# Matmuls that nobody reads, beside the first batch of an attention and feed-forward kernel

## The chip, the cores and the metric

The kernel runs on one core of one Trainium2 chip. The metric is the device time of one execution in microseconds (us); the median over runs counts. Engines are called TensorE (PE in the profile, PEld for its weight loads), VectorE (DVE), ScalarE (ACT), GpSimd (POOL) and SyncE (SP, whose queue issues nearly all DMAs here).

## The reference: what is computed

Attention on 8 batches of 8 heads, 576 tokens and 64 dimensions, as the sum of a coarse part (mean over 4 tokens, full softmax over 144 positions) and a local part (a window of 3 tokens to each side), followed by a feed-forward network with a leaky activation on 4608 rows:

```python
q_d = q.reshape(B, H, Sd, 4, D).mean(axis=3)      # k_d, v_d alike; Sd = 144
out_up = np.repeat(sm_attn(q_d, k_d, v_d), 4, axis=2)
mask = np.abs(pos[:, None] - pos[None, :]) < 4
out_local = softmax(where(mask, scale * q @ k.T, -1e9)) @ v
x = (out_up + out_local).transpose(0, 2, 1, 3).reshape(B * S, H * D)   # 4608 x 512
h = x @ w_in                                      # 512 x 2048
out = (maximum(h, 0) + alpha * minimum(h, 0)) @ w_out                  # 2048 x 512
```

w_in, w_out and alpha arrive as float64 and are decoded on the chip.

## The kernel before

**Feed-forward network.** The rows are cut into 18 chunks of 256 and the 2048 hidden columns into 8 pairs of 128, which makes 144 steps. A step `s` has these parts: `hidden` (24 matmuls of 128x256 into the tile `h`, line 784, from high and low parts `xh`, `xl` of x and `wih`, `wil` of w_in), `slopes` on ScalarE (tiles `t`, `sh`, lines 799 and 801), `larger` (line 811 on VectorE, or the helper `add` of line 76 on GpSimd for the steps in `EARLY`), `split` into `gh` (ScalarE, line 816) and `gl` (GpSimd, helper `sub`, line 73), and `product` (12 matmuls of 128x512 into `o`, line 845). In steps 0 to 21 GpSimd does both `larger` and `gl`.

**Weights.** Blocks `fp` of w_in and w_out are loaded (`load_raw`, lines 159 and 163, tile `raw`) into three slots in turn and decoded in `make`: ScalarE `Abs` (line 197, tile `temp`), four VectorE operations (201, 202, 206, 207), a ScalarE copy to `wih`/`woh` (212, 216) and a VectorE difference `wil`/`wol` (220, 224).

**First batch** (`first_batch`). Four pairs of heads. Per pair: TensorE transposes q and k (line 447, tiles `f0T`, `f1T`), ScalarE copies them to `qb`, `kT`; TensorE computes nine windows of scores (lines 463 and 467, tile `fs`); VectorE does the softmax (503 to 510, tile `fp`); TensorE transposes it (515, `fpt`), ScalarE copies (`fpT`), TensorE multiplies with v (531, `fpv`), and VectorE adds the coarse part (534, `fxs`) and splits x (540, 541, `xh`, `xl`). The coarse part runs beside it (`fsum`, `fsd`, `down_probs` with tile `pT`, `fdv`).

**Later batches.** `down(b, hp)` is the coarse part of one head pair of batch b: six loads (`ld`, line 247), folds on GpSimd (line 76, tiles `ld`, `s2q`, `s2k`, `s2v`), then `flip` (265, `qkT`), `scores` (278, `s`), the softmax (`dnb`, `dp`, `drs`), `turn` (302, `pT`) and `weigh` (312, `pv`). `local(u, ...)` is the local part of a third of a batch, unit u from 3 on; it runs on VectorE (lines 614 to 676) with a share on GpSimd (650, tile `pv`) and an exponential on ScalarE (634, tile `lex`).

**What sets the order.** Everything before event time 14 (`LISTED`) is put in order by a scheduler that has its own cost model of all engines; the rest stands in the order of a list of event times. Each engine works through its queue in order. So a change of TensorE's work in the first part can move instructions on every engine there.

In PSUM there are two banks `po` (`ps_o`), two `ph` (`ps_h`), two `d`, one `q` and one `l`.

Of the kernel before, what the change touches and what calls it, by code (L numbers as in the profile page):

```python
# [49 lines left out]
LISTED = 14  # L50
JOINS = (0.04, 0.06)


@with_exitstack
def tile_attention_moe(ctx: ExitStack, tc: tile.TileContext, q, k, v, w_in, w_out, alpha, out):
# [40 lines left out]
    for tag in ("spare6", "spare7", "spare2", "spare3", "slot2", "slot3"):  # L96
        one.tile([128, 2048], F32, tag=tag, name=f"{tag}_place")
    make_identity(nc, ident)

    masks = {}  # L100
# [136 lines left out]
    def down(b, hp, t0, gap, early=False):  # L237
# [21 lines left out]
        def flip():  # L259
            if hp == 0:  # L260
                new_od(b)
            pt = st["pt"] = bank("d", f"qkT{nm}")
            for i, x in enumerate("qk"):
                for g in range(2):
                    nc.tensor.transpose(pt[:, (2 * i + g) * 72:(2 * i + g) * 72 + 72], sums[x][:, g], ident[:72, :72])

        def operands():
# [7 lines left out]
        def scores():  # L275
            sv = st["sv"] = bank("d", f"s{nm}")[:96, 0:432].rearrange("p (b c) -> p b c", b=3)
            for bl in range(3):
                nc.tensor.matmul(sv[:, bl, :], qd32[:, bl, :], st["kd"], start=True, stop=True)  # L278

        def peak():  # L280
# [18 lines left out]
        def turn(g):  # L299
            tp = st["tp", g] = bank("d", f"pT{nm}_{g}")  # L300
            for bl in range(3):
                nc.tensor.transpose(tp[:72, 96 * bl:96 * bl + 96], st["p"][:, bl, 72 * g:72 * g + 72], ident[:96, :96])  # L302
# [36 lines left out]
    def down_probs(b, hp, sv):  # L339
# [16 lines left out]
        for g in range(2):  # L356
            tp = bank("d", f"pT{nm}_{g}")
            for bl in range(3):
                nc.tensor.transpose(tp[:72, 96 * bl:96 * bl + 96], p[:, bl, 72 * g:72 * g + 72],
                                    ident[:96, :96])  # L360
            th = one.tile([72, 288], F32, tag=f"th{g}", name=f"th{nm}_{g}")
            nc.scalar.copy(th, tp[:72, 0:288])
            parts.append(th)
            yield
# [20 lines left out]
    def first_batch(st):  # L385
# [13 lines left out]
        unit = st.tile([128, 128], F32R, name="unit")  # L399
        nc.scalar.copy(unit, ident)  # L400
        qb = st.tile([128, NWIN, 2, WIN], F32, name="qb")
        nc.vector.memset(qb[0:64, :, 1, :], 0.0)
# [38 lines left out]
        def pair(hp):  # L441
            halves = [slice(64 * e, 64 * e + 64) for e in range(2)]
            for x in range(2):
                for t0, nt in ((0, 4), (4, 4)):
                    ps = ps_h.tile([128, 512], F32, tag="ph", name=f"f{x}T{hp}{t0}")[:, 0:72 * nt]
                    for i in range(nt):
                        nc.tensor.transpose(ps[:, 72 * i:72 * i + 72],
                                            qk[hp][:, x, t0 + i].rearrange("p h d -> p (h d)"), ident[:72, :72])
                    if x == 0:
                        for e, r in enumerate(halves):  # L450
# [7 lines left out]
            for part in ("sd", "ds")[EM[hp] == "b"]:  # L458
                if part == "s":
                    banks = []  # L460
                    for w0, nw in ((0, 7), (7, 2)):
# [3 lines left out]
                        for i in range(nw):  # L465
                            w = w0 + i
                            nc.tensor.matmul(ps[:, KEYS * i:KEYS * i + KEYS], qb[:, w].rearrange("p e i -> p (e i)"),
                                             kT[:, WIN * w:WIN * w + KEYS], start=False, stop=(i == nw - 1))
                        banks.append((w0, w0 + nw, ps[:, 0:KEYS * nw].rearrange("p (w j) -> p w j", j=KEYS)))
                else:  # L470
# [9 lines left out]
                    for x in range(2):  # L480
                        for g in range(2):
                            nc.tensor.transpose(ps[:, (2 * x + g) * 72:(2 * x + g) * 72 + 72], sums[x][:, g],
                                                ident[:72, :72])
                    for e, r in enumerate(halves):
                        nc.scalar.mul(qd[r, :, 48 * e:48 * e + 48].rearrange("p b (i g) -> p b i g", g=2),
                                      ps[r, 0:144].rearrange("p (g b i) -> p b i g", g=2, b=3), DSCALE)
# [25 lines left out]
            for w0, nw in ((0, 4), (4, 4), (8, 1)):  # L512
                ps = pair_bank(FPT[hp][w0 // 4], f"fpt{hp}{w0}")
                for i in range(nw):
                    nc.tensor.transpose(ps[:KEYS, 128 * i:128 * i + 128], p[:, w0 + i], ident)
                nc.scalar.copy(pT[:, w0:w0 + nw].rearrange("p w i -> p (w i)"), ps[:KEYS, 0:128 * nw])
            if EM[hp] == "a":
                th = yield from down_probs(0, hp, sd)
            po = bank("d", f"fdv{hp}")
            for g in range(2):  # L520
                for e, r in enumerate(halves):
                    pr = th[g].rearrange("p (b e a) -> p b e a", b=3, e=2)[:, :, e]
                    nc.tensor.matmul(po[r, 0:144].rearrange("p (b a) -> p b a", b=3), vd[:, e, g], pr,
                                     start=(g == 0), stop=(g == 1))
            odf = st.tile([128, SD], F32, tag="odf", name=f"fod{hp}")
            nc.scalar.copy(odf, po[:, 0:144])
            for w0, nw in ((0, 4), (4, 4), (8, 1)):
                ps = pair_bank(FPV[hp][w0 // 4], f"fpv{hp}{w0}")
                for i in range(nw):
                    for e, r in enumerate(halves):  # L530
                        nc.tensor.matmul(ps[r, WIN * i:WIN * i + WIN], vw[hp][:, w0 + i, e, :],
                                         pT[:, w0 + i, 64 * e:64 * e + 64], start=True, stop=True)
                xs = rest[:, hp, :] if w0 == 8 else st.tile([128, 256], F32, tag="xs", name=f"fxs{hp}{w0}")
                nc.vector.tensor_tensor(
# [502 lines left out]
```

## Time and profile before

| | |
|---|---|
| median of 3 runs | 983.98 us (982.16 to 987.89) |
| the profiled execution: device time | 982.8 us |
| its span, first to last instruction | 981.0 us |
| TensorE busy (942.9 us of the span) | 96% |
| VectorE busy (819.5 us) | 84% |
| ScalarE busy (555.3 us) | 57% |
| GpSimd busy (527.6 us) | 54% |
| mean granted TensorE clock | 0.976 |

"Span" is taken from the first to the last instruction; the device time is 1.8 us longer. Shares are means over the whole span; the first 100 us, to which most of the change belongs, look different from the rest, so they are read in windows of their own. In a window table each engine has its busy time and its number of instructions, then come the granted TensorE clock (1.00 is full), the DMA share and the rate.

### The profile page before, as it was taken

The numbers are of one execution on the slowest core, as the hardware profiler recorded it, in microseconds if no ns is written. First come the engines' busy times: TensorE is split into PE (matmuls) and PEld (weight loads), VectorE is DVE, ScalarE is ACT, GpSimd is POOL, SyncE is SP. The second block draws the span as 40 slices with busy tenths as digits, with TensorE's granted clock in tenths as the row PEclk, the third lists the DMA queues.
The fourth block names the chain that finished last, engine by engine and source line by source line (L and its number), as shares of the span: only waits on it lengthen the run. The fifth ranks groups of instructions, "written<-read, shape, count | busy, mean of one in ns | idle before, by whom it ended". The sixth has DMA issues, their size and how long they took to land.

```text
span 981.0 us, 17943 instructions
## 1 busy us (share of the span) xinstructions
PE 942.9 (96%) x6402; PEld 842.0 (86%) x6402; DVE 819.5 (84%) x1318; ACT 555.3 (57%) x1483; POOL 527.6 (54%) x642
## 2 busy tenths in 40 slices
PE   5878999999999999999999999999999999999998
PEld 4757887987888888989988899898899989999997
DVE  7999978888879999998889899899898889997111
ACT  4767776544645655556554655565556664544442
POOL 2055877787887546555537365555466633323221
PEclk9956999999999999999999999999999999999999
DMA  8946723132333322422322423332333321310000
GB/s 200 232 146 208 254 90 107 61 114 85 111 101 116 114 76 88 139 80 83 119 78 86 127 86 93 108 98 68 105 112 103 110 63 46 97 34 22 1 22 22
DMA packets 63197, 98.28 MB, mean 100 GB/s; under 512 B 23556, under 2 KB 28932, under 8 KB 63108
## 3 DMA queue, kind: packets, MB, share of 16 engines
q1 hardware_dynamic: 62916, 96.88, 32.8%
q8 instruction: 50, 0.82, 0.3%
q10 hardware_dynamic: 192, 0.26, 0.1%
q14 instruction: 39, 0.32, 0.1%
HBM read 87.67 MB, written 9.44 MB: 99 GB/s over the span
## 4 chain that ended last, share of the span: by engine, by line
PE 59%; DVE 11%; POOL 4%; ACT 3%; issue 2%; DMA 1%; SPq 0%; DVEq 0%; POOLq 0%
PE o L845 28%; PE h L784 27%; DVE lb L673 3%; DVE pv L670 2%; DVE qk L614 1%; PE s L278 1%; PE pv L312 1%; DVE t L811 1%; DVE ls L618 1%; PE xp L682 1%; POOL t L76 1%; PE pT L302 1%; DVE xf L698 1%; ACT t L799 1%; POOL gl L73 1%
## 5 line engine op out<-in xcount | busy, mean ns | idle before, releaser
L73 POOL TENSOR_TENSOR gl<-t,gh 128x512 fp32r<-128x512 f32 x144 | 186.3, 1294 | 323.4 <-ACT gh L816 303.3
L799 ACT ACTIVATE t<-h,slope 128x256 f32<-128x256 f32 x288 | 136.3, 473 | 128.8 <-PE h L784 105.7
L845 PE MATMUL o<-woh,gh 128*128 128x512 f32 x576 | 192.8, 405 | 2.5 <-ACT gh L816 1.1
L784 PE MATMUL h<-xh,wih 128*128 128x256 f32 x1152 | 188.0, 285 | 2.6 <-ACT sh L801 1.9
L845 PE MATMUL o<-wol,gh 128*128 128x512 f32 x576 | 185.7, 393 | 0.0
L845 PE MATMUL o<-woh,gl 128*128 128x512 f32 x576 | 185.4, 393 | 0.0
L784 PE MATMUL h<-xh,wil 128*128 128x256 f32 x1152 | 180.7, 279 | 0.0
L784 PE MATMUL h<-xl,wih 128*128 128x256 f32 x1152 | 180.5, 279 | 0.0
L784 PEld LDWEIGHTS h<-xh,wih 128*128 128x128 f32 x1152 | 162.8, 190 | 13.0 <-ACT sh L801 2.6
L816 ACT CAST gh<-t 128x512 fp32r<-128x512 f32 x144 | 89.5, 622 | 140.3 <-DVE t L811 81.6
L76 POOL TENSOR_TENSOR ld<-ld 72x256 f32<-72x256 f32 x168 | 131.9, 787 | 67.4 <-DMA ld<-in_q 64.8
L784 PEld LDWEIGHTS h<-xh,wil 128*128 128x128 f32 x1152 | 155.3, 190 | 0.3
L784 PEld LDWEIGHTS h<-xl,wih 128*128 128x128 f32 x1152 | 154.6, 190 | 0.1
L811 DVE TENSOR_TENSOR t<-h,t 128x512 f32<-128x512 f32 x114 | 78.3, 687 | 88.2 <-ACT h L803 87.8
L618 DVE TENSOR_REDUCE ls<-qk 128x12 f32<-128x768 f32 (+1 forms) x126 | 136.2, 1083 | 3.1
L845 PEld LDWEIGHTS o<-woh,gl 128*128 128x128 f32 x576 | 108.0, 188 | 24.0
L845 PEld LDWEIGHTS o<-wol,gh 128*128 128x128 f32 x576 | 108.0, 188 | 23.1 <-DVE temp L207 0.2
L673 DVE TENSOR_TENSOR lb<-lb,pv 128x384 f32<-128x384 f32 x202 | 114.0, 564 | 5.9
L845 PEld LDWEIGHTS o<-woh,gh 128*128 128x128 f32 x576 | 99.1, 188 | 18.9 <-issue 2.6
L803 ACT ACTIVATE h<-h,sign 128x256 f32<-128x256 f32 x228 | 100.2, 439 | 0.0
L670 DVE TENSOR_TENSOR pv<-v,lb 128x1152 f32<-128x1152 f32 x84 | 93.6, 1115 | 2.7
L614 DVE TENSOR_TENSOR qk<-k,qp 128x768 f32<-128x768 f32 (+1 forms) x78 | 84.0, 1078 | 4.6 <-ACT qp L607 4.6
(151 smaller groups left out, 1185.7 us busy)
## 6 DMA issues: line engine op xcount, KB each, us to landing
k<-in_k SPq DMA_DIRECT2D x41, 384.0 KB
v<-in_v SPq DMA_DIRECT2D x41, 384.0 KB
out<-sg SPq DMA_DIRECT2D x140, 64.0 KB
raw<-in_moe_w_in SPq DMA_DIRECT2D x16, 512.0 KB
raw<-in_moe_w_out SPq DMA_DIRECT2D x16, 512.0 KB
ld<-in_q SPq DMA_DIRECT2D x56, 144.0 KB
ld<-in_k SPq DMA_DIRECT2D x56, 144.0 KB
ld<-in_v SPq DMA_DIRECT2D x56, 144.0 KB
```

The lines of the kernel that those rows point to most:

```text
L73: nc.gpsimd.tensor_tensor(o, a, b, op=ALU.subtract)
L76: nc.gpsimd.tensor_tensor(o, a, b, op=ALU.add)
L614: nc.vector.tensor_tensor(st["pr"][:, :nd], window(tiles[u, "k"], half, d0, nd), st["qp", half].unsqueeze(1).to_broadcast([128, nd, 2, 192 ...
L618: nc.vector.tensor_reduce(out=st["s"][:, half, d0:d0 + nd, :].rearrange("p a b -> p (a b)"), in_=st["pr"][:, :nd].rearrange("p a h (t d) - ...
L670: nc.vector.tensor_tensor(st["pr"][:, :nd], window4(tiles[u, "v"], half, d0, nd), prob(half, d0, nd), op=ALU.mult)
L673: nc.vector.tensor_tensor(st["acc"], st["acc"], st["pr"][:, i], op=ALU.add)
L784: nc.tensor.matmul(ph[:, j], w[:, m, 128 * o:128 * o + 128], x[:, m, :], start=(i == 0), stop=(i == 11))
L799: nc.scalar.activation(t[:, j], hs[st][:, j], AF.Copy, scale=slope[:, f:f + 1])
L803: nc.scalar.activation(other[:, j], hs[st][:, j], AF.Copy, scale=sign[:, f:f + 1])
L811: nc.vector.tensor_tensor(gs[st], hs.pop(st), gs[st], op=ALU.max)
L816: nc.scalar.copy(gh, t)
L845: nc.tensor.matmul(outs[c][m], g[:, j, 128 * m:128 * m + 128], wo[w][n][:, o, :], start=(f == 0 and i == 0), stop=(f == NF - 1 and i == 2))
```

## The change

Matmuls are added whose results nobody reads. A helper writes them to the columns of a PSUM tile that the kernel doesn't use, with operands that lie there anyway. They are put behind (in `turn`: ahead of) the matmuls of the stages of the first batch and of `down(1, 0)`, and 16 longer ones stand ahead of the first transposes.

```diff
+FILL = 3
+    def turn_over(ps, used, times):
+        w, x = turner["now"]
+        n = min(512 - used, x.shape[-1])
+        for _ in range(times):
+            nc.tensor.matmul(ps[:, used:used + n], w, x[:, 0:n], start=True, stop=True)
 # down(), only for the second batch's first pair (early)
 def flip():        +    turner["now"] = wi[0][0][:, 0, 0:128], wi[0][0][:, 0, 0:256]
                    +    turn_over(pt, 288, FILL)            # after the transposes
 def scores():      +    turn_over(full, 432, 2 * FILL)      # after the matmuls
 def turn(g):       +    turn_over(tp, 288, FILL)            # before the transposes
 # first batch
 down_probs:        +    turn_over(tp, 288, FILL)            # twice a pair
 first_batch:       +    turner["now"] = unit, wmask.rearrange("p w j -> p (w j)")
 pair(hp):
+                    if (hp, x, t0) == (0, 0, 0):
+                        for _ in range(16):
+                            nc.tensor.matmul(full.rearrange("p (a n) -> p a n", a=4), unit,
+                                             unit.unsqueeze(1).to_broadcast([128, 4, 128]), start=True, stop=True)
                     # f0T, f1T: four times a pair
+                    turn_over(full, 288, FILL)
 fs, w0 == 7:       +    turn_over(ps, 256, FILL)
 fsum:              +    turn_over(ps, 288, FILL)
 fpt, w0 == 8:      +    turn_over(ps, 256, FILL)
 fdv:               +    turn_over(po, 256, FILL)
 fpv: three times   +    turn_over(ps, 256, FILL)
```

Built, this gives TensorE 187 matmuls more: 16 of 128x512, 72 of 128x256 and 84 of 128x224 in the first batch, and 9 of 128x224 and 6 of 128x80 in `down(1, 0)`. Nothing is taken out. The other engines have the same instructions as before, in another order. The rows below are the program's own order, in which lines of the changed kernel are higher by 1 to 32 than those of the profile before (L107 is `turn_over`, L877 the old 845, L816 the old 784, L291, L319 the old 278, 302); a number at the end of a tile's name is that tile's own.

TensorE's first rows, before and after:

```order
L447 MATMUL f0T00_209<-ident_75,fqk0_154 128x72 x4
L447 MATMUL f0T04_216<-ident_75,fqk0_154 128x72 x4
L463 MATMUL fs00_254<-wmask_139,unit_141 128x490
L463 MATMUL fs07_263<-wmask_139,unit_141 128x140
L447 MATMUL f1T00_223<-ident_75,fqk0_154 128x72 x4
L447 MATMUL f1T04_229<-ident_75,fqk0_154 128x72 x4
```

```order
L468 MATMUL f0T00_209<-unit_141 128x512 x16
L471 MATMUL f0T00_209<-ident_75,fqk0_154 128x72 x4
L471 MATMUL f0T04_235<-ident_75,fqk0_154 128x72 x4
L107 MATMUL f0T00_209<-wmask_139,unit_141 128x224 x3
L107 MATMUL f0T04_235<-wmask_139,unit_141 128x224 x3
L488 MATMUL fs00_285<-wmask_139,unit_141 128x490
L488 MATMUL fs07_294<-wmask_139,unit_141 128x140
L471 MATMUL f1T00_245<-ident_75,fqk0_154 128x72 x4
L107 MATMUL f1T00_245<-wmask_139,unit_141 128x224 x3
L471 MATMUL f1T04_254<-ident_75,fqk0_154 128x72 x4
L107 MATMUL f1T04_254<-wmask_139,unit_141 128x224 x3
```

The sixteen long matmuls stand first, and each group of transposes has three short ones behind it.

GpSimd's queue where step 0 begins, before and after (`t0` is the sum for step 0; `ld1_1`, `s2k1_1`, `s2v1_1` are folds of the second batch's second pair):

```order
L76 TENSOR_TENSOR s2k1_1_1194<-ld1_1_3_1125 72x2x64
L76 TENSOR_TENSOR ld1_1_5_1201<-ld1_1_5_1201 72x2x128
L76 TENSOR_TENSOR t0_1019<-sh0_1020,t0_1019 128x512
L76 TENSOR_TENSOR s2v1_1_1248<-ld1_1_4_1157 72x2x64
L76 TENSOR_TENSOR s2v1_1_1248<-ld1_1_5_1201 72x2x64
L73 TENSOR_TENSOR gl0_1033<-t0_1019,gh0_1032 128x512
```

```order
L77 TENSOR_TENSOR s2k1_1_1375<-ld1_1_3_1306 72x2x64
L77 TENSOR_TENSOR ld1_1_5_1385<-ld1_1_5_1385 72x2x128
L77 TENSOR_TENSOR s2v1_1_1435<-ld1_1_4_1338 72x2x64
L77 TENSOR_TENSOR s2v1_1_1435<-ld1_1_5_1385 72x2x64
L77 TENSOR_TENSOR t0_1191<-sh0_1192,t0_1191 128x512
L74 TENSOR_TENSOR gl0_1208<-t0_1191,gh0_1207 128x512
```

`t0` now stands behind both folds `s2v1_1`.

TensorE around step 2 and the first product, before and after (`pT1_0`, `pv1_0` belong to the second batch's first pair, `qkT1_1` to its second):

```order
L302 MATMUL pT1_0_0_1197<-ident_75,dp1_0_1090 72x96
L302 MATMUL pT1_0_1_1203<-ident_75,dp1_0_1090 72x96
L784 MATMUL h2_1095<-xh0_107,wih1_854 128x256 x4
L784 MATMUL h2_1095<-xh0_107,wil1_855 128x256 x4
L784 MATMUL h2_1095<-xl0_108,wih1_854 128x256 x4
L784 MATMUL h2_1095<-xh0_107,wih1_854 128x256 x4
L784 MATMUL h2_1095<-xh0_107,wil1_855 128x256 x4
L784 MATMUL h2_1095<-xl0_108,wih1_854 128x256 x4
L312 MATMUL pv1_0_1243<-th1_0_0_1210,s2v1_0_940 64x144 x2
L312 MATMUL pv1_0_1243<-th1_0_1_1212,s2v1_0_940 64x144 x2
L265 MATMUL qkT1_1_1332<-ident_75,s2q1_1_1120 128x72 x2
L265 MATMUL qkT1_1_1332<-ident_75,s2k1_1_1194 128x72 x2
```

```order
L291 MATMUL s1_0_1242<-kd1_0_1238,qd32_100 96x144
L107 MATMUL s1_0_1242<-wih0_73 128x80 x6
L107 MATMUL pT1_0_0_1378<-wih0_73 128x224 x3
L816 MATMUL h2_1276<-xh0_107,wih1_1026 128x256 x4
L816 MATMUL h2_1276<-xh0_107,wil1_1027 128x256 x4
L816 MATMUL h2_1276<-xl0_108,wih1_1026 128x256 x4
L816 MATMUL h2_1276<-xh0_107,wih1_1026 128x256 x4
L816 MATMUL h2_1276<-xh0_107,wil1_1027 128x256 x4
L816 MATMUL h2_1276<-xl0_108,wih1_1026 128x256 x4
L877 MATMUL o0_0_1320<-woh0_79,gh0_1207 128x512
L877 MATMUL o0_0_1320<-wol0_80,gh0_1207 128x512
```

`pT1_0`, `pv1_0` and `qkT1_1` have left the place ahead of the first product `o0`; they now stand among the product matmuls of steps 1 and 2, behind the first product.

More of the change, by code (lines that the diff above doesn't have):

```diff
@@ L98, in tile_attention_moe @@
     make_identity(nc, ident)
+    turner = {}
+    def turn_over(ps, used, times):
[3 more added lines that the diff above has]
+            nc.tensor.matmul(ps[:, used:used + n], w, x[:, 0:n], start=True, stop=True)
     masks = {}
@@ L265, in flip @@
                     nc.tensor.transpose(pt[:, (2 * i + g) * 72:(2 * i + g) * 72 + 72], sums[x][:, g], ident[:72, :72])
+            if early:
+                turner["now"] = wi[0][0][:, 0, 0:128], wi[0][0][:, 0, 0:256]
+                turn_over(pt, 288, FILL)
         def operands():
@@ L275, in scores @@
         def scores():
-            sv = st["sv"] = bank("d", f"s{nm}")[:96, 0:432].rearrange("p (b c) -> p b c", b=3)
+            full = bank("d", f"s{nm}")
+            sv = st["sv"] = full[:96, 0:432].rearrange("p (b c) -> p b c", b=3)
             for bl in range(3):
                 nc.tensor.matmul(sv[:, bl, :], qd32[:, bl, :], st["kd"], start=True, stop=True)
+            if early:
+                turn_over(full, 432, 2 * FILL)
         def peak():
@@ L300, in turn @@
             tp = st["tp", g] = bank("d", f"pT{nm}_{g}")
+            if early:
+                turn_over(tp, 288, FILL)
             for bl in range(3):
@@ L360, in down_probs @@
                                     ident[:96, :96])
+            turn_over(tp, 288, FILL)
             th = one.tile([72, 288], F32, tag=f"th{g}", name=f"th{nm}_{g}")
@@ L400, in first_batch @@
         nc.scalar.copy(unit, ident)
+        turner["now"] = unit, wmask.rearrange("p w j -> p (w j)")
         qb = st.tile([128, NWIN, 2, WIN], F32, name="qb")
@@ L444, in pair @@
                 for t0, nt in ((0, 4), (4, 4)):
-                    ps = ps_h.tile([128, 512], F32, tag="ph", name=f"f{x}T{hp}{t0}")[:, 0:72 * nt]
+                    full = ps_h.tile([128, 512], F32, tag="ph", name=f"f{x}T{hp}{t0}")
+                    ps = full[:, 0:72 * nt]
+                    if (hp, x, t0) == (0, 0, 0):
+                        for _ in range(16):
+                            nc.tensor.matmul(full.rearrange("p (a n) -> p a n", a=4), unit,
+                                             unit.unsqueeze(1).to_broadcast([128, 4, 128]), start=True, stop=True)
                     for i in range(nt):
@@ L468, in pair @@
                                              kT[:, WIN * w:WIN * w + KEYS], start=False, stop=(i == nw - 1))
+                        if w0:
+                            turn_over(ps, 256, FILL)
                         banks.append((w0, w0 + nw, ps[:, 0:KEYS * nw].rearrange("p (w j) -> p w j", j=KEYS)))
@@ L483, in pair @@
                                                 ident[:72, :72])
+                    turn_over(ps, 288, FILL)
                     for e, r in enumerate(halves):
@@ L515, in pair @@
                     nc.tensor.transpose(ps[:KEYS, 128 * i:128 * i + 128], p[:, w0 + i], ident)
+                if w0 == 8:
+                    turn_over(ps, 256, FILL)
                 nc.scalar.copy(pT[:, w0:w0 + nw].rearrange("p w i -> p (w i)"), ps[:KEYS, 0:128 * nw])
@@ L524, in pair @@
                                      start=(g == 0), stop=(g == 1))
+            turn_over(po, 256, FILL)
             odf = st.tile([128, SD], F32, tag="odf", name=f"fod{hp}")
@@ L532, in pair @@
                                          pT[:, w0 + i, 64 * e:64 * e + 64], start=True, stop=True)
+                turn_over(ps, 256, FILL)
                 xs = rest[:, hp, :] if w0 == 8 else st.tile([128, 256], F32, tag="xs", name=f"fxs{hp}{w0}")
```

## The prediction

> **What bounds the kernel now.** I began with the slices of the page, TensorE, VectorE and the granted clock (each digit is a fortieth of the span, 24.5 us):
>
> ```profile
> PE   5878999999999999999999999999999999999998
> DVE  7999978888879999998889899899898889997111
> PEclk9956999999999999999999999999999999999999
> ```
>
> From the fifth slice on TensorE is full; in the first four, where the change lies, VectorE is fuller than TensorE. Then I cut the span where the granted clock changes (busy us and number of instructions for each engine, then clock, DMA share, GB/s):
>
> ```profile
> 0.00:32.76 32.76, 20.41 (x105) 18.49 (x106) 25.27 (x51) 17.33 (x41) 5.59 (x26) 1.00 0.91 195
> 32.76:46.41 13.65, 12.18 (x149) 9.86 (x149) 11.96 (x27) 11.83 (x35) 0.00 (x0) 1.00 1.07 287
> 46.41:87.37 40.96, 32.62 (x210) 25.57 (x207) 40.60 (x67) 28.74 (x71) 16.07 (x14) 0.50 0.48 158
> 94.20:97.61 3.41, 3.41 (x21) 3.18 (x20) 3.41 (x6) 1.46 (x3) 3.41 (x4) 0.50 0.91 282
> 97.61:230.70 133.09, 127.97 (x860) 112.98 (x856) 114.11 (x172) 84.41 (x230) 106.81 (x122) 1.00 0.38 125
> 230.70:250.00 19.30, 18.97 (x124) 17.31 (x125) 16.43 (x30) 8.05 (x26) 14.24 (x19) 0.91 0.22 67
> ```
>
> The clock is at half for 40.96 us of the first batch and for 3.41 us more. The 1.00 of the first row isn't believed, since the same score matmuls (first row below, 18 in 4.11 us) take 1.33 us for 10 once the clock is granted:
>
> ```profile
> 12.98 4.11 PE L467 MATMUL fs<-kT,qb 128*128 128x70 f32 x18
> 37.17 1.33 PE L467 MATMUL fs<-kT,qb 128*128 128x70 f32 x10
> ```
>
> So TensorE runs at about half speed until 32.8 us, and in all for about 77 of the first 97.6 us. What matters is who waits for it. VectorE's waits from 9.4 us, where the first pair begins, to 100 us (in all, times, longest; the list has no more rows):
>
> ```profile
> DVE fv L493 <- DMA fv<-in_v: 3.9, 2, 2.1
> DVE temp L201 <- ACT temp L197: 2.5, 3, 1.8
> ```
>
> Loads and a ScalarE operation, and no TensorE matmul. Between 46.41 and 87.37 VectorE is busy 40.60 of 40.96 us: its queue, pairs and weight decoding together, is the bound there, and a slow TensorE hides behind it. From 99 us on it is the reverse; the waits of TensorE between 99 and 229 us, and the largest of 229 to 300 us:
>
> ```profile
> PE o L845 <- ACT gh L816: 1.1, 1, 1.1
> PE o L845 <- ACT sg L851: 0.7, 1, 0.7
> PE h L784 <- ACT wih L212: 0.7, 1, 0.7
> PE o L845 <- ACT woh L216: 0.7, 1, 0.7
> ```
>
> ```profile
> PE qkT L265 <- ACT th L306: 3.9, 3, 2.2
> ```
>
> So the end is set by when the steps begin at about 99 us, by TensorE's work behind that, and by the few waits near 230 us. How the steps begin (rows of three engines, by start and length):
>
> ```profile
> 84.69 4.29 POOL L76 TENSOR_TENSOR ld<-ld 72x256 f32<-72x256 f32 x2 [21.64 <-DMA ld<-in_q]
> 92.19 0.45 ACT L801 ACTIVATE sh<-h,gain 128x256 f32<-128x256 f32 x1
> 97.36 1.29 POOL L76 TENSOR_TENSOR t<-sh,t 128x512 f32<-128x512 f32 x1
> 98.62 1.85 POOL L76 TENSOR_TENSOR s2v<-ld 72x128 f32<-72x128 f32 x2
> 98.69 0.62 ACT L816 CAST gh<-t 128x512 fp32r<-128x512 f32 x1 [3.03 <-POOL t L76]
> 99.36 0.51 PE L845 MATMUL o<-woh,gh 128*128 128x512 f32 x1 [1.05 <-ACT gh L816]
> ```
>
> `sh` of step 0 is ready at 92.64, but GpSimd works at folds in its queue until 97.36; `t`, `gh` and the first product follow one another. TensorE's speed isn't in this chain; GpSimd's queue is.
>
> **The change part by part.** *The 187 matmuls.* Their price comes from rows at both clocks, 256 columns first at half, then at full:
>
> ```profile
> 94.99 1.05 PE L784 MATMUL h<-xh,wil 128*128 128x256 f32 x4
> 95.84 1.05 PE L784 MATMUL h<-xl,wih 128*128 128x256 f32 x4
> 272.83 2.73 PE h L784 x24
> 275.57 2.74 PE o L845 x12
> ```
>
> From start to start that is 0.85/4 = 0.21 us at half clock, and 2.73/24 = 0.114 us at full; 512 columns take 2.74/12 = 0.23 us. The 156 short ones of the first batch are then 18 us at full clock, at most 33 us at half; per pair of heads, 39, that is 4.4 to 8.3 us. The cover is VectorE's full queue. The 16 long ones take 3.7 us at full clock and 7.3 at half. They need `unit` (ready at 2.45 us by the first row below) and end at 9.8 us at the latest; the first transposes stood at 9.23, waiting for their load. That is 0.5 us late at worst, and VectorE's next need of TensorE, the maximum of the scores, begins without a wait behind `wil` at 18.94. I take 0.
>
> ```profile
> 2.15 0.30 ACT L400 CAST unit<-ident 128x128 fp32r<-128x128 f32 x1
> 9.23 1.19 PE L447 MATMUL f0T<-ident,fqk 72*128 72x72 f32 x8 [9.23 <-DMA fqk<-in_q]
> 18.94 0.87 DVE L503 TENSOR_REDUCE fmx<-fs 128x7 f32<-128x490 f32 x2
> ```
>
> [...]
>
> *Order on VectorE and ScalarE up to 40 us.* ScalarE's first two `woh` copies move back, behind four copies of the third pair, and VectorE's `wol` behind them; two sums of q move up into VectorE's longest wait for `fv`, 2.1 us.
>
> ```profile
> 29.46 1.34 ACT L216 ACTIVATE woh<-temp,sign 128x512 fp32r<-128x512 f32 x2 [1.90 <-DVE temp L207]
> ```
>
> If VectorE fills that wait, it comes out up to 2.1 us earlier; if it waits for the copies instead, later by about their 1.34 us. I take 0, since the wait for `fv` stays in the queue.
>
> *Order where the steps begin.* `t` of step 0 now stands behind the two folds `s2v`, so it comes 1.85 us later, and `gh`, the first product and step 3 (whose bank is freed behind `gh` in ScalarE's queue) with it. `sh` of step 0 moves behind the copy `wih` of a weight block; it has 4.7 us between 92.64 and 97.36 for that: nothing. TensorE fills the wait with nothing new, since `pT1_0`, `pv1_0` and `qkT1_1`, which ran ahead of 99.36, now come behind the first product, where TensorE is full. By the rows below (`pv` from a place at full clock) they cost 0.66 + 0.71 + 0.48, and three short fills 0.34: 2.2 us.
>
> ```profile
> 90.16 0.66 PE L302 MATMUL pT<-ident,dp 96*72 96x96 f32 x6
> 97.83 0.35 PE L265 MATMUL qkT<-ident,s2q 72*128 72x72 f32 x2
> 98.02 0.29 PE L265 MATMUL qkT<-ident,s2k 72*128 72x72 f32 x2
> 132.47 0.71 PE L312 MATMUL pv<-th,s2v 72*64 72x144 f32 x8
> ```
>
> So TensorE is late by 1.85 + 2.2 = 4.05 us at step 3. *What takes it back:* TensorE waits 2.2 us once for `th` near 230, and the 0.91 clock of 230.70 to 250 costs it 0.09 x 19.3 = 1.7 us: up to 3.9 us of slack, if ScalarE and VectorE are not late there too. The new order favours them: ScalarE's decode operations (197, 212, 216) move ahead of the steps' own, and VectorE's waits for ScalarE in the decoding shrink. Between 0 and 3.9 I take half, 2.
>
> Sum: 0 + 0 + 4.05 - 2.0 = +2.05 us on the profiled execution's 982.8. The median of the runs shown lies 1.2 us above that execution, so the forecast is 983.98 + 2.05, rounded to 986 us. Half a per cent, 4.9 us, is about what a measurement of this kernel can tell from no change.
>
> **The rivals.**
> (a) *TensorE's clock is what the first batch lacks*: every matmul there shortens and the steps begin earlier. For it: 77 us at half clock. Against it: VectorE waits for no matmul. What could still be won is in step 2's second half (12 matmuls at 0.21 for 0.114: 1.2 us), the 1.7 us of the low clock near 230 and the 2.2 us wait there, if GpSimd comes through its folds in time: 5.1 us, so 978.9. It decides if `t` of step 0 starts before 97.4 us. [...]
> (b) *The lag is not taken back, and step 11 adds to it.* In the new order the exponential of unit 3 (`lex`) stands ahead of `gh` of step 11 and the slopes of step 12 on ScalarE, and its products `pv` ahead of `gl` of step 11 on GpSimd. Before:
>
> ```profile
> 163.82 1.30 POOL L73 TENSOR_TENSOR gl<-t,gh 128x512 fp32r<-128x512 f32 x1 [0.70 <-ACT gh L816]
> 168.89 0.63 PE L845 MATMUL o<-woh,gh 128*128 128x512 f32 x2
> 169.95 1.62 POOL L650 TENSOR_TENSOR pv<-v,lex 128x384 f32<-128x384 f32 x2
> ```
>
> That moves `gl` from 163.8 to 171.6 at the earliest. Its end moves from 165.1 to 172.9; the product of step 11 began at 168.9 (second row) and is 4 us late now, so it just fits; each microsecond by which unit 3 comes later than before goes straight to TensorE. With nothing taken back (+2.0) and 3 us here the time is 991. It decides when unit 3's `pv` starts behind 170 us.
> (c) *The fills don't raise the clock and crowd TensorE.* Then about 90 of them lie in the 40.96 us stretch at 0.21 us: 19 us beside the 32.62 us that were busy, 10.7 more than it holds; 983.98 + 10.7 + 2 = 997. Against it: with TensorE that full the clock rose at 87.37.
> (d) *The clock stays low and nothing happens*: the fills fit into TensorE's gaps, 986 as forecast, since the order is the same.
>
> **How the numbers follow.** The forecast gets 0.55 (its own range 982 to 989), (d) 0.07, (a) 0.14, (b) 0.18, (c) 0.06. Faster by over 0.5% is (a), 0.14; slower is (b) and (c), 0.24; the rest, 0.62, is within 0.5%. The range from 979 to 991.5 leaves out about half of (a), all of (c) and a third of (b), 0.19.
>
> **What would show it.** The first batch's last `xl` is the mark for VectorE:
>
> ```profile
> 90.32 0.95 DVE L541 TENSOR_TENSOR xl<-fxs,xh 128x256 fp32r<-128x256 f32 x1
> ```
>
> Right: a clock of 1.00 over most of 10 to 97 us, VectorE still busy over 0.95 of 46 to 87 us and without a wait for TensorE, `t` of step 0 at about 99 us, the first product at about 101, TensorE full behind it, and a shorter wait for `th` near 230. Wrong: VectorE reaching that `xl` more than 2 us earlier, which would mean that TensorE was in its path after all; or waits of TensorE for `gh` or `sh` between 120 and 180 us of more than 3 us together, which would be (b).

## The result, and the profile after

The changed kernel takes 989.56 us (median of 10 runs, 988.20 to 991.08) against 983.28 (10 runs, 981.84 to 988.08) before: a ratio of 1.0052 [1.0034, 1.0070] over all runs (the two medians alone give 1.0064). The forecast was 986.0, in a range of 979 to 991.5: the time lies in the range, 3.6 us above the forecast. Runs of one kernel spread by 3 us (the changed kernel) to 13 us here, so a profiled execution can lie some us off its kernel's median; where it does, I say so.

The profiled execution takes 989.6 us (span 987.8, against 982.8 and 981.0). The slices of the changed kernel's page, and its instruction queue (packets, MB, share of time):

```profile
PE   7979899999899999999999999999999999999998
DVE  6999689689869999988989899899898889997111
PEclk8997899999999999999999999999999999999999
...
q8 instruction: 52, 0.85, 0.4%
```

The clock's first four digits are 8, 9, 9, 7 (9, 9, 5, 6 before, where the first was not to be believed). The windows of the prediction, and two short ones in which the clock is low:

```profile
46.41:87.37 40.96, 33.69 (x284) 28.63 (x283) 40.02 (x64) 28.72 (x67) 20.30 (x12) 0.80 0.47 155
97.61:230.70 133.09, 127.91 (x860) 114.67 (x859) 105.69 (x166) 84.16 (x234) 102.82 (x118) 0.97 0.39 124
101.70:108.53 6.83, 5.29 (x20) 4.90 (x21) 3.31 (x7) 5.96 (x19) 4.27 (x4) 0.52 1.03 335
265.90:269.31 3.41, 3.41 (x18) 3.41 (x18) 2.21 (x3) 1.37 (x4) 2.60 (x4) 0.52 0.52 177
```

Between 46.41 and 87.37 the granted clock is 0.80 (0.50 before), and VectorE is as full as it was, 40.02 of 40.96 us. VectorE's waits from 9 to 101 us:

```profile
DVE temp L210 <- ACT temp L206: 2.5, 2, 1.5
DVE fqk L502 <- PE f0T L471: 1.8, 1, 1.8
DVE wol L233 <- ACT woh L225: 0.9, 1, 0.9
DVE fv L521 <- DMA fv<-in_v: 0.6, 1, 0.6
DVE dnb L362 <- PE fsd L519: 0.5, 1, 0.5
```

Two waits for TensorE are new, 2.3 us together, and the waits for `fv` shrank from 3.9 to 0.6. Against the kernel before, the faster TensorE gave VectorE nothing. Where the time went, by the starts of the same instructions in both traces (us):

| | before | changed | later by |
|---|---|---|---|
| last `xl` of the first batch | 90.32 | 90.38 | 0.06 |
| SyncE issues the loads `ld<-in_q` | 80.03 | 81.38 | 1.35 |
| GpSimd's folds of them begin | 84.69 | 88.76 | 4.07 |
| `t` of step 0 | 97.36 | 101.27 | 3.91 |
| first product | 99.36 | 103.24 | 3.88 |
| first matmul with `gl`, step 0 | 102.85 | 108.75 | 5.90 |
| the same, step 4 | 123.40 | 131.61 | 8.21 |
| the same, step 21 | 237.68 | 241.81 | 4.13 |
| the same, step 25 | 264.60 | 271.46 | 6.86 |
| end of the span | 981.0 | 987.8 | 6.8 |

VectorE's part ends on time in this execution. The loss begins on SyncE's queue and GpSimd, grows behind the first product, is half taken back, and 2.7 us more are lost near 265 us. The rows of its first part, before and then changed (start, length; SPq is the issue of a DMA):

```profile
79.17 0.81 SPq L163 DMA_DIRECT2D raw<-in_moe_w_out  x2
80.03 0.81 SPq L247 DMA_DIRECT2D ld<-in_q  x2
```

```profile
80.51 0.83 SPq L172 DMA_DIRECT2D raw<-in_moe_w_out  x2
81.38 1.17 SPq L256 DMA_DIRECT2D ld<-in_q  x2
...
88.76 2.29 POOL L77 TENSOR_TENSOR ld<-ld 72x256 f32<-72x256 f32 x2 [19.46 <-DMA ld<-in_q]
...
100.45 0.86 POOL L77 TENSOR_TENSOR s2v<-ld 72x128 f32<-72x128 f32 x2
101.27 1.27 POOL L77 TENSOR_TENSOR t<-sh,t 128x512 f32<-128x512 f32 x1
...
103.24 0.80 PE L877 MATMUL o<-woh,gh 128*128 128x512 f32 x1 [5.17 <-ACT gh L848]
```

The block of w_out ahead of the loads in SyncE's queue is issued 1.34 us later, and the loads with it. From issue to the first fold it takes 7.38 us instead of 4.66. The folds `s2v`, ahead of `t` now, cost only 0.86 us. TensorE then waits 5.17 us for `gh`, the only wait of it from 99 to 230 us, and from about 102 us, within this wait, the clock is at half for 6.83 us (third window above).

### The profile page after: what moved, and what is told of

It is laid out like the page before. It is cut to its first block, busy times and chain, and to the rows that moved or that the text cites. A ratio compares the mean times of both kernels' runs of the same rounds, so it can differ in the third digit from the quotient of the medians.

```text
span 987.8 us, 18319 instructions
## 1 busy us (share of the span) xinstructions
PE 956.6 (97%) x6589; PEld 859.3 (87%) x6589; DVE 815.7 (83%) x1318; ACT 555.7 (56%) x1483; POOL 532.0 (54%) x642
## 4 chain that ended last, share of the span: by engine, by line
PE 56%; DVE 14%; POOL 4%; ACT 3%; issue 2%; DMA 1%; SPq 0%; DVEq 0%; POOLq 0%; ACTq 0%
PE o L877 26%; PE h L816 25%; DVE lb L705 3%; DVE pv L702 2%; DVE qk L646 2%; DVE ls L650 2%; DVE t L843 2%; PE s L291 1%; PE pv L329 1%; PE xp L714 1%; POOL t L77 1%; DVE xf L730 1%; ACT t L831 1%; PE pT L319 1%; POOL gl L74 1%
## 5 line engine op out<-in xcount | busy, mean ns | idle before, releaser
L831 ACT ACTIVATE t<-h,slope 128x256 f32<-128x256 f32 x288 | 136.3, 473 | 124.6 <-PE h L816 101.9
L877 PE MATMUL o<-woh,gh 128*128 128x512 f32 x576 | 193.1, 405 | 5.2 <-ACT gh L848 5.2
L816 PE MATMUL h<-xh,wih 128*128 128x256 f32 x1152 | 187.8, 284 | 1.0 <-ACT sh L833 0.8
L877 PE MATMUL o<-wol,gh 128*128 128x512 f32 x576 | 186.6, 394 | 0.0
L877 PE MATMUL o<-woh,gl 128*128 128x512 f32 x576 | 186.1, 393 | 0.0
L816 PE MATMUL h<-xh,wil 128*128 128x256 f32 x1152 | 181.8, 279 | 0.0
L816 PE MATMUL h<-xl,wih 128*128 128x256 f32 x1152 | 180.4, 279 | 0.0
L816 PEld LDWEIGHTS h<-xh,wih 128*128 128x128 f32 x1152 | 163.3, 190 | 10.9 <-issue 1.2
L77 POOL TENSOR_TENSOR ld<-ld 72x256 f32<-72x256 f32 x168 | 134.3, 802 | 65.8 <-DMA ld<-in_q 64.5
L816 PEld LDWEIGHTS h<-xh,wil 128*128 128x128 f32 x1152 | 155.7, 190 | 0.4
L816 PEld LDWEIGHTS h<-xl,wih 128*128 128x128 f32 x1152 | 154.5, 189 | 0.5 <-issue 0.2
L877 PEld LDWEIGHTS o<-woh,gl 128*128 128x128 f32 x576 | 108.1, 188 | 23.9 <-issue 0.2
L877 PEld LDWEIGHTS o<-wol,gh 128*128 128x128 f32 x576 | 108.1, 188 | 22.8 <-issue 0.2
L877 PEld LDWEIGHTS o<-woh,gh 128*128 128x128 f32 x576 | 99.3, 189 | 21.0 <-ACT gh L848 5.4
```

What stands on the lines that cost most here:

```text
L77: nc.gpsimd.tensor_tensor(o, a, b, op=ALU.add)
L816: nc.tensor.matmul(ph[:, j], w[:, m, 128 * o:128 * o + 128], x[:, m, :], start=(i == 0), stop=(i == 11))
L831: nc.scalar.activation(t[:, j], hs[st][:, j], AF.Copy, scale=slope[:, f:f + 1])
L877: nc.tensor.matmul(outs[c][m], g[:, j, 128 * m:128 * m + 128], wo[w][n][:, o, :], start=(f == 0 and i == 0), stop=(f == NF - 1 and i == 2))
```

## The experiments

In each kernel below the order is written out: for every engine a list of ranks (`PLAN`) says in which order the instructions are issued, by links that set the order of issue and wait for nothing. "Old order" is that of the kernel before, "new order" that of the changed one, so order and matmuls can be had apart. All were timed beside the kernel before.

### Order and matmuls apart

**All 187 matmuls in the old order.** Each added matmul stays with the real one that it belongs to.

```diff
+PLAN = {
+    'PE': [(0, 8), (23, 1), (31, 1), (8, 10), (24, 7), (32, 2), (71, 4), (18, 2), (75, 4), (20, 3),
...
+    for engine, plan in PLAN.items():
+        row = [i for first_, n_ in plan for name in real[first_:first_ + n_] for i in with_fills[name]]
+        for a_, b_ in zip(row, row[1:]):
+            tc.add_manual_dep(b_, a_.name, mybir.DependencyInfo(
+                mybir.DependencyClass.NoSync, mybir.DependencyReason.DATA), reason="row")
```

> All 187 added matmuls, but every engine's queue in the order of the kernel before (each added matmul stands behind the matmul it was written behind). Theory A, the order of the queues costs the time and the matmuls cost nothing: t of step 0 at 97 to 98 us, first product at about 99.4, and 980 to 984 us in all, since the granted clock is high where it was low in the first batch. Rival B, the matmuls themselves cost: they lie in TensorE's way in the first batch and beside steps 0 to 3, and the time stays at 987 to 990 us.

Measured: 991.84 us (990.17 to 995.51), 1.0080 [1.0053, 1.0106]. VectorE's waits from 9 us on, the largest of some 6.5 us for TensorE, and the last `xl`:

```profile
DVE rest L576 <- PE fpv L115: 1.6, 2, 0.8
DVE fxs L576 <- PE fpv L115: 1.0, 1, 1.0
DVE fqk L512 <- PE f1T L481: 1.0, 1, 1.0
```

```profile
98.77 0.67 DVE L583 TENSOR_TENSOR xl<-fxs,xh 128x256 fp32r<-128x256 f32 x1
```

L115 is the added matmul itself. `xl` comes 8.4 us late, and the steps are later by the same 8.2 us from step 0 to step 4. So VectorE's queue does not hide the matmuls by itself: in the order of before they cost 8 us.

**The new order without the matmuls.**

```diff
+PLAN = {
+    'PE': [(0, 8), (23, 1), (31, 1), (8, 10), (24, 7), (32, 2), (71, 4), (18, 2), (94, 1), (102, 1),
...
-    def turn_over(ps, used, times):
...
-                turn_over(tp, 288, FILL)
...
-                    turn_over(full, 288, FILL)
```

> None of the added matmuls, but every engine's queue in the order of the changed kernel. Theory A (order): 986 to 990 us, with t of step 0 at 99.5 to 101.5 us and TensorE waiting over 4 us for the first gh. Rival B (the matmuls cost): 982 to 985 us.

Measured: 986.05 us (983.25 to 987.79), 1.0016 [1.0001, 1.0031]; the profiled execution took 987.35, 1.3 over that median. How its steps begin:

```profile
101.44 1.26 POOL L84 TENSOR_TENSOR t<-sh,t 128x512 f32<-128x512 f32 x1
```

```profile
103.40 0.79 PE L854 MATMUL o<-woh,gh 128*128 128x512 f32 x1 [2.74 <-ACT gh L825]
```

The steps begin as late as in the changed kernel, with no matmul added. Here the loads were issued at 82.40, 2.37 us later than before, and the folds `s2v` ahead of `t` took 1.84 us: the new order alone is enough for it. In this order VectorE does wait for the slow TensorE, 4.0 us up to 101 us, the most of it for scores:

```profile
DVE fmx L512 <- PE fs L476: 2.9, 3, 1.7
```

With the matmuls it waits 2.3 us, so here the faster clock takes some of the waits away; no gain in time is shown by that, since the last `xl` starts at 91.67 us without them and, in traces of this order with all of them ahead of it, between 90.38 and 93.20. The four medians:

| | no matmuls | all 187 |
|---|---|---|
| old order | 983.9 | 991.84 |
| new order | 986.05 | 989.56 |

By the medians the matmuls cost 8.0 us in the old order and 3.5 in the new; the new order costs 2.2 by itself and saves 2.3 once they are there. The cost of the matmuls is clear of noise in both orders. The order is not: by itself its ratio is 1.0016 [1.0001, 1.0031], barely off no change, and with the matmuls the intervals of the two orders overlap. That the matmuls cost more in the old order is seen in VectorE's rows too (6.5 against 2.3 us).

### Which matmuls hold VectorE up

**The 16 long ones alone**, old order (`FILL = 0`):

```diff
-FILL = 3
+FILL = 0
```

> The order of the kernel before, and of the added matmuls only the 16 long ones ahead of the first transposes. Theory C, the short ones of the first batch stand in TensorE's queue ahead of what VectorE needs next: the long ones alone cost nothing, 982 to 985 us, and VectorE waits for TensorE less than 1 us up to 100 us. Rival, the long ones keep the clock wrong or the first transposes late: 986 to 992 us.

**The 156 short ones of the first batch alone**, old order:

```diff
-            if early:
+            if False:
...
-                        for _ in range(16):
+                        for _ in range(0):
```

> The order of the kernel before, and of the added matmuls only the 156 short ones of the first batch. Theory C: they alone bring the loss that all 187 bring in this order, 989 to 993 us; VectorE waits for TensorE 4 to 8 us up to 100 us, and the last xl of the first batch starts at 96 to 100 us. Rival, the 15 beside the second batch's first pair or the 16 long ones bring it: 983 to 986 us.

Measured: 985.12 us (982.62 to 989.94), 1.0016 [0.9994, 1.0038], and 990.98 us (986.35 to 999.06), 1.0055 [1.0034, 1.0077]. VectorE's waits for TensorE in the first are one row:

```profile
DVE fqk L512 <- PE f1T L481: 0.5, 1, 0.5
```

In the second they sum to 8.0 us, in an execution of 999.06, the longest of its kernel:

```profile
DVE fqk L512 <- PE f0T L481: 4.0, 3, 1.7
DVE rest L576 <- PE fpv L115: 1.2, 2, 0.9
DVE fxs L576 <- PE fpv L115: 1.0, 1, 1.0
```

The last `xl` starts at 90.90 in the first and at 101.94 in the second, 11.6 us late; the waits for TensorE are the largest part of that, not all of it. The long ones are hidden, in TensorE's wait for its first loads (no cost is clear of noise); the short ones between the real matmuls are not.

**The 156 short ones ahead of their stage's real matmuls** instead of behind, old order, the others left out as in the run before. Behind them, a reader of the tile waits for the added matmuls too, as they write the same tile: of the 751 signals that TensorE gives to semaphores in the changed program, 50 come from an added matmul. Ahead, none does, while TensorE has the same work. The edit at the transposes `f0T`, `f1T` (the other stages alike; `True` marks matmuls that go ahead):

```diff
+                    turn_over(full, 288, FILL, True)
...
-                    turn_over(full, 288, FILL)
```

> As the run before with the 156 short matmuls in the old order, but each group of them ahead of the real matmuls of its stage and not behind them. Behind, the readers of a PSUM tile wait for the last matmul written to it, which is an added one (48 waits in the program with all 187); ahead, they wait for the real one, and TensorE does the added ones while it waits for its operands. Theory C1, it is this wait for matmuls that nobody reads that costs: VectorE's waits for TensorE up to 100 us fall from 8 to under 3 us, the last xl starts at 90 to 94 us, 983.5 to 987 us in all. Rival C2, TensorE's time alone costs, wherever the matmuls stand: 989 to 993 us, as behind.

Measured: 989.95 us (987.14 to 994.33), 1.0065 [1.0037, 1.0094]. VectorE still waits 6.3 us for TensorE:

```profile
DVE fqk L512 <- PE f1T L482: 2.6, 2, 2.1
DVE fqk L512 <- PE f0T L482: 1.7, 1, 1.7
DVE rest L576 <- PE fpv L573: 1.3, 2, 1.1
```

So it is mostly TensorE's time, not the wait on the shared tile: the real matmuls stand behind the added ones either way. The intervals of this version and the one before it overlap, and the two profiled executions are the shortest of the one and the longest of the other, so a small share of the shared tile isn't excluded.

**All 187 with 32 columns**, in both orders, to take TensorE's time away and keep the rest.

```diff
-        n = min(512 - used, x.shape[-1])
+        n = 32
```

> All 187 added matmuls in the order of the kernel before, each with 32 columns in place of 80 to 512: as many instructions, the same places and the same waits, a fraction of TensorE's time, and hardly a reason for the clock to rise. Theory F, it is TensorE's time in front of what VectorE needs next that costs: 984 to 987 us, and VectorE waits for TensorE under 3 us up to 100 us. Rival G, their number and their places (waits that name them, blocks of instructions fetched elsewhere) cost: 989.5 to 992.5 us, as with the wide ones.

> All 187 added matmuls in the changed kernel's own order, each with 32 columns. Theory F: as this order without them, 985 to 987.5 us. Rival G: as the changed kernel, 988.5 to 990.5 us.

Measured: 1013.28 us (1010.13 to 1014.26), 1.0278 [1.0251, 1.0306], in the old order and 1011.97 (1009.35 to 1012.79), 1.0261 [1.0231, 1.0291], in the new. The premise failed: the narrow ones are not short. Two rows of TensorE in the old order, and one window:

```profile
10.67 0.80 PE L115 MATMUL f0T<-wmask,unit 128*128 128x32 f32 x3
11.31 0.74 PE L480 MATMUL f0T<-ident,fqk 72*128 72x72 f32 x4
...
75.16 3.95 PE L501 MATMUL fs<-kT,qb 128*128 128x70 f32 x18
```

```profile
46.00:76.00 30.00, 30.00 (x199) 27.90 (x198) 15.49 (x32) 13.53 (x34) 3.31 (x6) 1.00 0.24 82
```

From start to start one takes 0.64/3 = 0.213 us, as much as 256 columns at half clock (0.21). And the real matmuls stay at half speed long after: 18 `fs` still take 3.95 us at 75 us (4.11 before, at half), so the 1.00 of the window isn't believed. TensorE is busy all of its 30.00 us and VectorE 15.49: TensorE has become the bound, VectorE waits 26.1 us for it up to 130 us (23.6 in the new order). What the pair shows is rival (c), in full. It can't tell what shorter matmuls would do.

### How the steps begin

The first three of these four are the changed kernel, in its order, with one edit each.

**Without the 39 of the third pair.**

```diff
-        for _ in range(times):
+        for _ in range(0 if turner.get("pair") == 2 else times):
```

> The changed kernel in its own order, without the 39 added matmuls of the third pair of heads. Theory A1, the loads of the second batch's second pair land 2.5 us late because TensorE's 16 KB block of instructions at 82.3 us, fetched by DMA, falls among the w_out loads ahead of them: 39 matmuls fewer move that fetch 4 to 5 us later, the folds start at 86 to 87 us and not at 88.8, t of step 0 at about 99, and the time is 2 to 3 us less, 986.5 to 987.5. Rival: the loads land late because SyncE issues them late or because of TensorE's or VectorE's pace; the folds start at 88.8 again and the time is 989 to 990.

Measured: 987.49 us (984.59 to 989.95), 1.0025 [1.0008, 1.0041]; the profiled execution is the shortest, 984.59.

```profile
81.44 0.81 SPq L266 DMA_DIRECT2D ld<-in_q  x2
...
86.49 1.91 POOL L86 TENSOR_TENSOR ld<-ld 72x256 f32<-72x256 f32 x2 [18.73 <-DMA ld<-in_q]
...
99.57 1.25 POOL L86 TENSOR_TENSOR t<-sh,t 128x512 f32<-128x512 f32 x1
```

The loads are issued when the changed kernel issues them and land 5.05 us later, not 7.38. What differs is a transfer of the instruction queue (q8). Its packets have 16,384 bytes, 50 of them before and 52 in the changed kernel, one per 128 and 127 matmuls of TensorE; so I take each for a fetch of TensorE's program code. The fetch at 82.3 us in the changed kernel, in the middle of the w_out block that goes ahead of the loads, comes at 90.5 here, with fewer matmuls ahead of it. Over the traces of this study, with a fetch inside that transfer the loads took 7.38, 6.5, 6.52, 6.43 and 5.73 us from issue to first fold; without one, or with one in the last 0.7 us, 4.66 to 5.05 (six traces). So of the 4.07 us by which the folds were late, 1.35 are the later issue and up to 2.7 the fetch.

**TensorE kept busy before the first product**: 20 more matmuls into the bank that step 0's product then overwrites, behind `hidden` of step 2.

```diff
+        if st == 0:
+            for _ in range(20):
+                one_more = nc.tensor.matmul(outs[0][0], wi[0][0][:, 0, 0:128], xT[0][0][:, 0:2].rearrange("p a n -> p (a n)"),
+                                            start=True, stop=True)
```

> The changed kernel in its own order, with 20 matmuls of 128x512 more that nobody reads, between step 2's hidden and the first product, into that product's own bank: they fill the 5.2 us that TensorE waits there. Theory A2, that wait costs the clock too (half for 6.8 us from 101.7, that is 2.6 us of TensorE's time behind the first product): the clock stays at 1.00 from 88 us on and the time is 2 to 3 us less, 986.5 to 987.5. Rival: the lost clock is taken up by waits that exist anyway behind it: 989 to 990.

Measured: 987.26 us (986.52 to 990.81), 1.0030 [1.0011, 1.0049]: 2.3 us less than the changed kernel by the medians. Its window behind 91 us has the full clock, and the first product waits 0.58 us:

```profile
91.00:120.00 29.00, 26.84 (x182) 23.87 (x181) 23.11 (x30) 18.41 (x45) 24.86 (x23) 1.00 0.70 239
```

```profile
106.14 0.50 PE L893 MATMUL o<-woh,gh 128*128 128x512 f32 x1 [0.58 <-ACT gh L859]
```

In this execution the first product comes 2.9 us later than in the changed kernel (the loads were issued 3.7 us later, and VectorE waited 4.1 us for `fv`), yet from there to the end it takes 881.38 us instead of 884.55. Of these 3.2 us, 2.4 lie between the first product and step 4, where the bridge works; the rest comes from other places between 230 and 265 us. So matmuls that nobody reads can pay, where TensorE itself waits on the path. The intervals of this version and of the changed kernel overlap; the trace and the medians point the same way.

**`t0` ahead on GpSimd.** The difference in its queue, by the tiles written (the number is the step's, `1_1` the second batch's second pair):

```diff
+t0
 ld1_1_3
 ld1_1_4
+gl0
+t1
 s2k1_1
 ld1_1_5
 s2v1_1
 s2v1_1
-t0
-gl0
-t1
```

> The changed kernel with one thing moved: on GpSimd t and gl of step 0 and t of step 1 stand ahead of most folds of the second batch's second pair (t behind the first fold s2k, then one ld fold, another, gl, t of step 1). Nothing left out. Theory D, GpSimd's queue, which waits for the late loads, is the last link of what is lost where the steps begin: t of step 0 at 94 to 97 us, the first product at 98 to 99.5, TensorE waits under 1.5 us there and its clock stays full, 982 to 985.5 us. Rival: what is won there is lost by 130 us, since the weights are decoded no earlier: 987 to 990 us.

Measured: 987.03 us (985.29 to 990.46), 1.0027 [1.0008, 1.0046]; the profiled execution, 990.46, is the longest. `t` starts at 97.42, the first product 3.0 us earlier than in the changed kernel:

```profile
100.24 0.39 PE L888 MATMUL o<-woh,gh 128*128 128x512 f32 x1
```

By step 8, at about 160 us, some 2 of these 3.0 us are given back, where the delayed folds and the work behind them make TensorE wait:

```profile
PE o L888 <- ACT woh L235: 1.3, 2, 1.2
PE pT L329 <- ACT dp L322: 0.6, 1, 0.6
```

Near 265 us this execution loses 2.7 us in the way that the changed kernel does (told below): a code fetch at 261.1 falls on its stores. The 2.5 us by which its median is below the changed kernel's is less than was expected.

**The kernel before with its steps earlier**: no added matmul, old order, but `sh` of step 0 ahead of an `Abs` and `gh` ahead of `th` on ScalarE, the first product's `gh` matmuls ahead of `pv1_0`, `qkT1_1` on TensorE, and on GpSimd:

```diff
+t0
 s2k1_1
+gl0
 ld1_1_3
 ld1_1_4
+t1
 s2k1_1
 ld1_1_5
-t0
 s2v1_1
 s2v1_1
-gl0
-t1
```

It is the version that the reading so far asks for.

> The kernel before, without added matmuls, with three queues changed: ScalarE does sh of step 0 ahead of the Abs of the next weight block and gh of step 0 ahead of the copies th; GpSimd does t, gl of step 0 and t of step 1 ahead of folds; TensorE does the four gh products of step 0 ahead of pv1_0 and qkT1_1. Theory D: what sets the end is when the steps begin; the first product at 94 to 97 us in place of 99.4, and 978.5 to 982 us. Rival, the decoding of the weights on VectorE sets the pace up to 130 us: TensorE waits for wih, wil, woh or wol 2 to 5 us more between 100 and 140 us, and the time is 982.5 to 985 us.

Measured: 986.91 us (982.21 to 989.72), 1.0022 [1.0000, 1.0044]: no gain. The first product at 98.40 is only 1 us earlier than before, and two new waits of TensorE follow up to 130 us:

```profile
PE o L854 <- POOL gl L81: 1.6, 1, 1.6
PE qkT L274 <- POOL s2k L84: 0.6, 1, 0.6
```

Earlier steps starve where GpSimd feeds them: at step 4 they are 3.6 us later than before. No version here beat the kernel before.

### The late loss

At 258 to 266 us the changed kernel's rows are these (SyncE, ScalarE, TensorE), and before them the two that answer to the first and last in the kernel before:

```profile
254.18 4.18 SPq L854 DMA_DIRECT2D out<-sg  x8
...
259.75 0.34 PE L265 MATMUL qkT<-ident,s2q 72*128 72x72 f32 x2 [1.42 <-ACT th L306]
```

```profile
258.31 5.03 SPq L886 DMA_DIRECT2D out<-sg  x8
...
263.46 0.47 ACT L833 ACTIVATE sh<-h,gain 128x256 f32<-128x256 f32 x1 [1.00 <-DMA out<-sg]
...
264.99 0.35 PE L274 MATMUL qkT<-ident,s2q 72*128 72x72 f32 x2 [2.54 <-ACT th L323]
```

A code fetch at 260.3 us falls on the stores; one of the eight issues takes 1.29 us instead of 0.42, ScalarE waits 1.00 for a store, TensorE 1.1 more for `th`. Behind that wait the clock is at half for 3.41 us (fourth window), worth 1.7. Together 2.8, against 2.7 lost. To shift the fetch, the 15 matmuls of `down(1, 0)` are left out, new order (the edit stands at three places):

```diff
-            if early:
+            if False:
```

> The changed kernel in its own order, without the 15 added matmuls beside the second batch's first pair. Theory E, the number of matmuls sets when each 16 KB block of TensorE's instructions is fetched: in the changed kernel the block at 260.3 us falls on the store of the third chunk's output (an issue of SyncE takes 1.29 in place of 0.42 us, sh waits 1.0 us for the store, TensorE waits 2.5 us for th and not 1.4, and its clock falls to half for 3.4 us): 15 matmuls fewer move the fetch 2 us on, behind that store, and the time is 2.5 to 3.3 us less, 986 to 987.2. Rival, the half-clock stretch and the longer wait at 265 us come from elsewhere: only the 0.3 us of three matmuls go, 989 to 990 us.

Measured: 988.94 us (986.16 to 991.76), 1.0050 [1.0028, 1.0072].

```profile
260.76 4.16 SPq L897 DMA_DIRECT2D out<-sg  x8
...
266.31 0.34 PE L284 MATMUL qkT<-ident,s2q 72*128 72x72 f32 x2 [1.42 <-ACT th L333]
```

With the fetch at 267.6 the stores and the wait are as before, and the steps behind have 2.6 us back. But a half-clock stretch appears at 238.4 to 241.9, and the first folds came 1.3 us later still (a fetch on the w_out block at 81.7). The collision is shown; that removing it makes the kernel faster is not: the median is 0.6 us below the changed kernel's, where 2.5 to 3.3 were expected. Nor does each collision cost: in the changed trace a store's issue takes 1.74 us at 413.6, beside a fetch at 413.7, and the steps are 6.84 us later than before both ahead of it (step 40) and behind it (step 60).

## Why the prediction was right or wrong

The sign and the range held, but the change is about three times the forecast's: 6.3 us by the medians, 6.8 in the profiled pair, against 2.05. The sum had four errors, one of them of the other sign; without that one, 2.1 us, the profiled execution would stand at 991.7, outside the range. So the range held with some luck. Measured in the profiled pair: 3.9 (first product) + 2.0 (half clock behind it) + 2.3 (moved matmuls) − 4.1 + 2.7 (near 265 us) = 6.8.

**"The cover is VectorE's full queue": right for the changed kernel, wrong as an argument.** The last `xl` moved by 0.06 us and VectorE waited 2.3 us for TensorE. (In two more traces with the same matmuls in the same order up to there, those of the bridge and of `t0` ahead, it starts at 93.20 and 92.80; single traces don't tell how much of that is chance.) But "VectorE waits for no matmul" says only that each real matmul has some slack, not that 4 to 8 us per pair fit ahead of it: in the old order they cost 8 us, and the changed kernel's order goes with a smaller cost. The forecast had costed the order for itself, not as the place that the scheduler found for the matmuls. The price was low too. From start to start, the three of a group of 256 columns took 0.289 us each at half clock and 0.157 at full in the changed trace, on average, not 0.21 and 0.114: the first of a group took 0.36 to 0.38 at half clock and 0.20 to 0.22 at full, the next one the forecast's price. So 156 cost some 23 to 43 us, not 18 to 33. The 16 long ones, 3.7 to 7.3 us by the forecast, took 5.71:

```profile
2.50 5.71 PE L468 MATMUL f0T<-unit 128*128 128x512 f32 x16 [2.50 <-ACT unit L418]
```

**"`t` of step 0 comes 1.85 us later": the right queue, half the size.** The two folds cost 0.86. The rest I did not look for: the loads that the folds wait for are issued 1.35 us later, since the w_out block ahead of them is, and landed 2.7 us later, beside a code fetch; the folds between ran 1.0 us faster than before, which makes 3.9. That step named GpSimd's queue and took its input as fixed. "Order up to 40 us: 0" may be the term behind the 1.35: the order without matmuls issues those loads late too (82.40). It isn't shown, since three traces of the old order without the short matmuls issue them at 80.03, 80.63 and 81.77.

**"TensorE fills the wait with nothing new": true, and its consequence missed.** TensorE was empty for 5.17 us, and the clock was at half for 6.83 us from 101.9 on, 2.0 us lost by the first `gl` matmul. The 20 bridging matmuls gave 2.3 us back by the medians. In the trace TensorE does nothing in the 3.41 us ahead of the drop, and 6.83 is two times 3.41. Elsewhere the clock dropped behind 3.41 us in which TensorE was busy for 0.87 to 1.54 us (last section). The forecast put no half clock behind this wait.

**"`pT1_0`, `pv1_0`, `qkT1_1` and three fills, 2.2 us": right.** From the first `gl` matmul to step 4 the lag grows from 5.90 to 8.21.

**"Half of the slack takes back 2.0": too low.** 4.1 us are back by step 21. Three waits of 0.7 us (for `sg`, `wih`, `woh`) are gone, and so is the half clock at 230.7 us, forecast at 1.7; the lag falls by 1.4 there. The third source, a shorter wait for `th` near 230, did not come.

**What no step held: the 2.7 us near 265 us.** The code fetch there stands at 264.7 us before, behind the stores, and at 260.3 in the changed kernel, among them; the late half-clock stretch begins at 230.7 and at 265.8.

**The rivals.** (a) fell: the clock rose (from 0.50 to 0.80 between 46.41 and 87.37 us) and nothing was gained; by its own condition `t` had to start before 97.4 and started at 101.27. (b)'s waits of TensorE between 120 and 180 us did not appear. (c) describes the narrow matmuls, not this kernel; in the old order the matmuls crowd TensorE too, but there the clock rose (0.91 between 46.5 and 87.5 us). (d) fell, as the clock rose. "A clock of 1.00 over most of 10 to 97 us" came about, with half clock left at 16.7 to 23.4, 61 to 64.2 and 74.7 to 88.2; so did VectorE's busy share (40.02 of 40.96 us). The other signs of being right did not: VectorE waited for TensorE, `t` and the first product came 2 us later than named, TensorE ran at half clock behind the product, and the wait for `th` near 230 is no shorter.

**Open.** In the profiled pair of changed kernel and new order alone, the lag at step 21 is the same (4.13 and 4.37) and all 2.2 us between them arise at 253 to 271. So in this pair the matmuls cost nothing until the collision near 265 us. That this holds for the medians' 3.5 us, and what makes runs of one kernel differ by 3 to 13 us, isn't shown. Most rows here come from one execution of each kernel; six traces of the new order (the narrow matmuls aside) issue the loads anywhere from 81.38 to 85.12.

## What to carry to other kernels

Idle work on TensorE paid here where TensorE waits on the path that sets the end (20 matmuls ahead of the first product, at a clock of 1.00 behind them: 2.3 us by the medians, with intervals that overlap), and cost where other engines set the pace and need its real matmuls soon (8 us in the old order). Before an addition is called hidden, its length is to be held against the slack of each consumer, not against the share of busy time; and where a scheduler reorders, order and addition are tried apart, because one can mask the other. A late start is followed back past the engine's queue to the issue of the loads that feed it.

## What the runs showed of the hardware

- The instruction queue q8 moved 50 packets of 16,384 bytes before and 52 in the changed kernel, one per 128 and 127 matmuls of TensorE (6402 and 6589); from one packet to the next 101 to 158 matmuls start. They are taken for TensorE's program code for that reason. With one inside the transfer of the w_out block the loads took 5.73 to 7.38 us from issue to first fold, otherwise 4.66 to 5.05. Before and in the changed kernel, the 8 issues of stores on SyncE that took over 0.9 us (0.42 is the median of 140, 1.87 the longest) had a fetch within 0.8 us of their start.
- A matmul of 128x32 with these operands took 0.213 us, as long as one of 256 columns at half clock; PEld was busy 27.90 of 30.00 us there. With these among the real ones in the old order, the matmuls of `hidden` still took 0.21 us each up to 117 us and 0.11 behind, though TensorE was busy for 91.5 of the 93 us before. The profile shows it busy for 30.00 of 30.00 us, at a clock of 1.00, where the real matmuls ran at half speed (18 `fs` in 3.95 us): its busy time didn't tell the speed there.
- The clock also dropped behind 3.41 us in which TensorE was not empty: it was busy in them for 1.54 us before (90.8 to 94.2), 0.87 in the changed kernel (262.4 to 265.8) and 1.40 in the new order alone, where a wait of 2.74 us was followed by 6.83 us at half clock.
- Late half-clock stretches, 3.41 us each, stood elsewhere from trace to trace: 230.7 us before, 265.8 in the changed kernel, 237.5 with the bridge, 238.4 without the 15 of `down(1, 0)`; three traces have none from 110 to 350 us (without the 39 of the third pair, the new order alone, the 156 short ones ahead).
